# One kernel, one issue order: the order of all engines from a fixed table, and two first-tile pieces made into one

## The chip, the cores and the metric

The kernel runs on one core of a Trainium2 chip. The metric is the device time of one execution in microseconds (us). "Span" is the time from the first to the last instruction in a trace. All executions quoted here are at a granted TensorE clock of 0.997 to 1.000.

Engine names in the profile: PE is TensorE, PEld its weight loads, DVE is VectorE, ACT is ScalarE, POOL is GpSimd, SP is SyncE, which issues most DMAs (SPq).

## The reference, cut to what matters

```python
xn = _layernorm(x)                        # x: 1 x 2048 x 512, bf16
q, k, v = heads(xn@wq), heads(xn@wk), heads(xn@wv)   # paraphrased: 32 heads of 16, 4 segments of 512
for s in range(4):
    p = _softmax(qs @ ks.T * scale + mask)           # causal within the segment
    a_dot = p @ vs
    pq = phi(qs)                                     # phi(t) = t+1 if t>0 else exp(t)
    a_mem = (pq @ M) / (pq @ z + 1e-6)
    o = g * a_mem + (1.0 - g) * a_dot
    M, z = M + phi(ks).T @ vs, z + phi(ks).sum()
return x + concat(o) @ wo + silu(xn @ w1) @ w2       # w1: 512 x 1792, w2: 1792 x 512
```

## The kernel before

All work is written as tasks, each on one engine, with dependencies and with buffers that it takes and frees. A small scheduler in Python decides, while the program is built, in which order each engine issues its tasks. At run time each engine only follows its list. In the kernel before, the scheduler simulates the engines and picks by due times, which a table named SHIFT corrects by hand.

```python
            if e == "PE":
                s = [t for t in c if t.kind == "score"]
                if s:
                    return min(s, key=lambda t: t.seq)
# ... cut: PV blocks, ScalarE's and VectorE's rules
            return min(c, key=lambda t: (t.due, t.seq))
# ... cut
                    if t.lock:
                        other = "DVE" if e == "POOL" else "POOL"
                        d += max(0.0, port[other] - now)
                        port[e] = now + d
```

The last four lines matter later: the simulation holds a VectorE task marked `lock` while a GpSimd task marked so runs, and the other way round.

The heads of the first key and query tiles are made in four pieces of 128 columns each, so that the first scores can start early:

```python
        for j in (2 * hf, 2 * hf + 1):
            c, o = slice(j * P, (j + 1) * P), slice((j % 2) * P, (j % 2) * P + P)
            def f(c=c, o=o):
                for ki in range(DT):
                    mm(b.tile[:, o], w[:, ki, 0:P], xnT_b[0].tile[:, ki, c], ki == 0, ki == DT - 1)
            pcs.append(A("PE", 0.3, f, [xnT_done[0][j], loads], due + 0.01 * j, takes=(b,),
                         frees=(b, xnT_b[0]), mode="full", label=label))
```

The normalisation of the attention output multiplies by R, which comes back through DRAM. It is the task `a_t`, four per segment (three in the last).

```python
            def f_a(dt=dt, rb=rb):
                v = N_b[s].tile[:, dt, :]
                nc.vector.tensor_tensor(out=v, in0=v, in1=rb.tile[:], op=ALU.mult)
            a = A("DVE", 0.34, f_a, [d4] + mg, due_rep, frees=(rb, N_b[s]), label="a_t", lock=True)
```

The softmax here doesn't subtract the row's maximum and nothing guards it: scores larger than these inputs give would overflow.

Of the kernel before, what the change touches and what calls it, by code (L numbers as in the profile page):

```python
# [14 lines left out]
P = 128  # L15
# [25 lines left out]
STARVE = 0.55  # L41
# [4 lines left out]
LOWB = 1  # L46
# [8 lines left out]
LAST = 1  # L55
PVW = 0.0
# [9 lines left out]
SW = 0.1  # L66
SEM = 0.05
SHIFT = {
    "POOL": {
        ("", 4): -31.1, ("kB", 16): 80.6, ("pq", 0): -10.1, ("pq", 2): 18.3, ("pq", 6): 8.4,  # L70
        ("pq", 10): 6.2, ("M52", 1): -7, ("Mbf", 2): 35.4,
    },
    "PE": {
        ("tr", 1): 9.5, ("k1", 0): -13.1, ("k2", 0): 22.9, ("q2", 0): -12.4, ("q3", 0): -0.3,
        ("h0.0", 0): -54.5, ("h0.2", 0): 30.1, ("h0.3", 0): -7.3, ("h0.6", 0): 11.6,
        ("h0.7", 0): 10.6, ("h0.12", 0): -10.2, ("k4", 0): -0.9, ("q6", 0): 9.6, ("k7", 0): -11.8,
        ("v10", 0): -5.8, ("v11", 0): -6.8, ("M0", 0): 5, ("w2.1", 0): 1.8, ("w2.3", 0): -1.8,
        ("wo.3", 0): 20.3, ("h1.1", 0): 7.4, ("h1.3", 0): -16.4, ("h1.4", 0): 3.5,
        ("h1.5", 0): 1.8, ("h1.6", 0): 10.2, ("h1.7", 0): -10.6, ("h1.8", 0): -3.7,
        ("k8", 0): -7.8, ("v22", 0): -12.9, ("M1", 0): -7, ("psN", 0): -5.6, ("w2.4", 0): -30.2,  # L80
        ("w2.7", 0): -3.9, ("wo.4", 0): 28.9, ("wo.5", 0): 3.2, ("wo.6", 0): -27.6,
        ("wo.7", 0): -42.5, ("PV8", 0): 5.8, ("PV9", 0): 8.6, ("PV10", 0): 7.3, ("h2.0", 0): -7.2,
        ("h2.1", 0): 10.7, ("h2.5", 0): -7.9, ("h2.6", 0): -13.3, ("h2.9", 0): 7.9,
        ("q12", 0): -2.8, ("q13", 0): 4.8, ("k14", 0): 1.6, ("k15", 0): 15, ("v32", 0): 26.1,
        ("M2", 0): 29, ("w2.10", 0): 4, ("wo.9", 0): -27.9, ("wo.10", 0): 17.9, ("PV12", 0): 31.2,
        ("PV13", 0): 47.7, ("h3.0", 0): -14.7, ("h3.1", 0): 46.3, ("h3.2", 0): 38.7,
        ("h3.4", 0): -37.3, ("h3.7", 0): 26.5, ("h3.10", 0): -7.1, ("h3.12", 0): 16.4,
        ("h3.13", 0): 40.6, ("outT2", 0): -24.2,
    },
    "DVE": {  # L90
        ("stats", 3): 4.5, ("stats", 10): -3.1, ("xn", 5): -0.9, ("k0", 0): 11.1,
        ("EO", 26): 36.4, ("glu", 45): -20.7, ("tailA", 1): 4.6,
    },
    "SP": {
        ("Z", 15): -16.3, ("Z", 26): 8.7, ("den", 12): -6.9, ("den", 17): 3.5, ("den", 18): -28.9,
        ("den", 20): -20.5, ("out", 10): 21.7, ("mg", 14): 26.1,
    },
}


class Task:
    __slots__ = (
        "eng", "dur", "vis", "fn", "due", "nwait", "ready", "outs", "takes", "frees", "kind",
        "mode", "seq", "started", "end", "tvis", "label", "lock",
# [19 lines left out]
class Ring:  # L124
# [4 lines left out]
    def count(self, t):  # L129
        return sum(1 for a in self.at if a <= t + 1e-9)  # L130

    def take(self, t):
        i = min(range(len(self.at)), key=lambda k: self.at[k])
        assert self.at[i] <= t + 1e-9
        self.at[i] = float("inf")
        return i


class Sched:
    ENGS = ("SP", "ACTQ", "PE", "ACT", "DVE", "POOL")  # L140

    def __init__(self):
        self.tasks = []
        self.log = None
        self.names = {}

    def add(self, eng, dur, fn, deps=(), due=0.0, vis=None, seqdeps=(), takes=(), frees=(),
            kind="", mode=None, keep=0, label="", lock=None):
        t = Task()
        t.eng, t.dur, t.fn, t.due, t.kind, t.mode = eng, dur, fn, due, kind, mode  # L150
# [11 lines left out]
        t.started = False  # L162
        t.seq = len(self.tasks)
        t.label = label
# [9 lines left out]
    def shift(self, table):  # L174
        seen = {}
        for t in self.tasks:
            key = (t.eng, t.label)
            if t.eng == "PE" and t.label not in ("k0", "q0", "tr"):
                n = 0
            else:  # L180
                n = seen.get(key, 0)
                seen[key] = n + 1
            t.due += table.get(t.eng, {}).get((t.label, n), 0.0)

    def run(self):
        free = {e: 0.0 for e in self.ENGS}
        pool = {e: [] for e in self.ENGS}
        for t in self.tasks:
            if t.nwait == 0:
                pool[t.eng].append(t)  # L190
        port = {"DVE": 0.0, "POOL": 0.0}
        left = len(self.tasks)
        now = 0.0
        order = []
        st = {"mode": "full", "exp_next": None, "exps": 0}
        nexps = sum(1 for t in self.tasks if t.kind == "exp")

        def can(t):
            return all(b.idx is not None or b.ring.count(now) > keep for b, keep in t.takes)

        def pick(e):
            c = [t for t in pool[e] if t.ready <= now + 1e-9 and can(t)]
            if not c and e == "PE" and LAST:
                c = [
                    t for t in pool[e] if t.ready <= now + 1e-9 and t.kind == "" and all(
                        b.idx is not None or b.ring.count(now) > 0 for b, _ in t.takes)
                ]
            if not c:
                return None
            if e == "PE":  # L210
                s = [t for t in c if t.kind == "score"]
                if s:
                    return min(s, key=lambda t: t.seq)
                pv = [t for t in c if t.kind == "pv"]
                if not pv and any(
                    t.kind == "pv" and t.ready <= now + 1e-9 and t.due + PVW < now for t in pool[e]
                ):
                    c = [t for t in c if not any(
                        b.idx is None and b.ring is self.names["banks"] for b, _ in t.takes)]
                    if not c:  # L220
                        return None
                if pv:
                    b = min(pv, key=lambda t: (t.due, t.seq))
                    if st["mode"] != "full" or b.due < now:
                        return b
                    c = [t for t in c if t.kind != "pv"]
                    if not c:
                        return b
                return min(c, key=lambda t: (t.due, t.seq))
            if e == "ACT":  # L230
                s = [t for t in c if t.kind == "exp"]
                if s:
                    return min(s, key=lambda t: t.seq)
                b = min(c, key=lambda t: (t.due, t.seq))
                if st["exps"] < nexps and st["exp_next"] is not None:
                    late = 0.06
                    if not any(
                        t.kind != "score" and t.ready <= now + 1e-9 and can(t) for t in pool["PE"]
                    ):
                        late = STARVE  # L240
                    if now + b.dur > st["exp_next"] + late:
                        return None
                return b
            if e == "DVE":
                bk = self.names["banks"]
                if bk.count(now) <= LOWB:
                    f = [t for t in c if any(b.ring is bk for b in t.frees)]
                    if f:
                        return min(f, key=lambda t: (t.due, t.seq))
            return min(c, key=lambda t: (t.due, t.seq))  # L250

        while left:
            for e in self.ENGS:
                while free[e] <= now + 1e-9:
                    t = pick(e)
                    if t is None:
                        if e == "PE" and self.log is not None:
                            self.log.append((now, [
                                (x.label, round(x.ready, 1), [n for n, r in self.names.items() for b, k in x.takes if b.ring is r and b.idx is None and r.count(now) <= k])
                                for x in sorted(pool["PE"], key=lambda x: (x.due, x.seq))[:6]]))  # L260
                        break
                    pool[e].remove(t)
                    d = t.dur
                    if e == "PE":
                        if t.mode != st["mode"]:
                            d += SW
                            st["mode"] = t.mode
                        else:
                            pass
                    if t.lock:  # L270
                        other = "DVE" if e == "POOL" else "POOL"
                        d += max(0.0, port[other] - now)
                        port[e] = now + d
                    t.started = True
                    t.end = now + d
                    t.tvis = now + t.vis + (d - t.dur)
                    free[e] = t.end
                    for b, keep in t.takes:
                        if b.idx is None:
                            b.idx = b.ring.take(now)  # L280
# [1198 lines left out]
```

## Time and profile before

The time is 226.51 us, the median of 3 executions (226.26 to 226.98). The attention loop consists of 72 score blocks S0 to S71. Each is a short burst of row-tiled matmuls, followed on TensorE by about ten 512-column matmuls, or by a block of the attention's PV product, or by both. If one knows what each kind costs, the start times of the 72 blocks give a ledger: whatever an interval lasts beyond its content is a stall. The prediction derives the five unit costs from the intervals.

| part of the span, before | us |
|---|---|
| to S0 | 11.43 |
| S0 to S71, work | 187.35 |
| S0 to S71, stalls (S23 0.81, S27 0.42, S28 0.58, S42 0.55, S46 0.84, S47 0.27, S49 0.21, S62 0.14, rest -0.1) | 3.72 |
| after S71, work on TensorE | 19.51 |
| last eviction and output | 3.49 |
| span | 225.5 |

A stall of "S28" is time lost between the start of block 28 and that of block 29.

### The profile page before, as it was taken

To read this page: it belongs to the slowest core of one execution; us is meant where nothing else is said; L and a number is where in the kernel's file an instruction comes from. 1 tells how busy PE (TensorE), PEld (TensorE's weight loads), DVE (VectorE), ACT (ScalarE), POOL (GpSimd) and SP (SyncE) were. 2 spreads that over 40 slices of the span, in tenths; PEclk is the share of its full clock that TensorE was granted. 3 is DMA by queue.
4 is the path that set the end of the run, shared out by engine and by line. 5 is a ranking of instruction groups with operands and counts; after the bars stand their busy time and mean duration, and the time that the engine had idled before them with its cause. 6 is when DMAs were issued, how large, how long until landed. Compare 5 with 4: busy or idle time off the path is not lost.

```text
span 225.5 us, 6740 instructions
## 1 busy us (share of the span) xinstructions
PE 213.4 (95%) x2757; PEld 101.1 (45%) x2792; DVE 173.2 (77%) x305; ACT 179.7 (80%) x165; POOL 162.3 (72%) x283
## 2 busy tenths in 40 slices
PE   6899999999999898999999999999999999999994
PEld 6634444435443444444444334344554444444441
DVE  3788988879994789789976849988665784775873
ACT  4498999999988799988989787899898787994000
POOL 4779998889987678999984775968797644568100
PEclk9999999999999999999999999999999999999999
DMA  6974458550265432050364350020523201123202
GB/s 191 366 235 115 99 143 208 65 177 3 47 86 126 93 102 100 22 166 1 49 149 86 71 96 24 0 73 6 178 60 69 97 3 47 55 76 89 74 3 94
DMA packets 30708, 21.11 MB, mean 94 GB/s; under 512 B 15956, under 2 KB 29780, under 8 KB 30676
## 3 DMA queue, kind: packets, MB, share of 16 engines
q1 hardware_dynamic: 29860, 20.14, 34.4%
q10 hardware_dynamic: 816, 0.52, 0.8%
q8 instruction: 22, 0.36, 0.7%
q14 instruction: 10, 0.08, 0.1%
HBM read 11.73 MB, written 2.64 MB: 64 GB/s over the span
## 4 chain that ended last, share of the span: by engine, by line
PE 66%; DVE 8%; ACT 7%; DMA 7%; POOL 5%; issue 4%; SPq 1%; ACTq 0%; POOLq 0%
PE ps L583 54%; PE psS L583 11%; ACT Pt L947 6%; DMA phiK<-pkT 2%; POOL Pt L966 2%; DMA dR<-Zr 2%; DMA R<-dR 1%; POOL kB L824 1%; DMA x_all<-in_A_x_dram 1%; DVE xn L696 1%; DVE pq L760 1%; POOL rstd L685 1%; ACT hT L1239 1%; DVE st L662 1%; DMA Zg<-dZ 1%
## 5 line engine op out<-in xcount | busy, mean ns | idle before, releaser
L947 ACT ACTIVATE Pt<-psS 128x2048 bf16<-128x2048 f32 x72 | 135.4, 1880 | 18.3 <-PE psS L583 15.3
L966 POOL TENSOR_SCALAR_AFFINE_SELECT Pt<-Pt 64x512 bf16<-64x512 bf16 (+1 forms) x144 | 91.2, 634 | 29.3 <-ACT Pt L947 22.1
L583 PE MATMUL ps<-xnT,w 128*128 128x512 bf16 x214 | 57.0, 380 | 0.8 <-issue 0.5
L1243 DVE SCALAR_TENSOR_TENSOR hT<-hT,ps 128x512 bf16<-128x512 bf16 x56 | 36.9, 676 | 15.6 <-ACT hT L1239 15.4
L583 PE MATMUL ps<-w,hT 128*128 128x512 bf16 x185 | 46.6, 380 | 1.5 <-issue 1.4
L1239 ACT ACTIVATE hT<-ps 128x512 bf16<-128x512 f32 x56 | 32.1, 601 | 0.3 <-PE ps L583 0.3
L583 PEld LDWEIGHTS <-hT 128*128 128x128 bf16 x224 | 20.2, 98 | 24.5 <-issue 2.0
L583 PE MATMUL psS<-qT,kB 32*128 32x256 bf16 (+5 forms) x640 | 28.7, 261 | 1.7 <-ACT Pt L947 1.3
L583 PEld LDWEIGHTS <-w 128*128 128x128 bf16 x224 | 19.7, 98 | 23.3 <-issue 2.4
L583 PEld LDWEIGHTS <-kB 32*128 32x128 bf16 x640 | 12.0, 92 | 28.8 <-issue 27.2
L824 POOL TENSOR_SCALAR kB<-kT,pm 128x512 bf16<-128x512 bf16 x30 | 21.8, 736 | 4.1 <-DVE kT L819 2.6
L583 PE MATMUL ps<-Pt,V 64*32 64x256 bf16 (+5 forms) x640 | 19.8, 260 | 0.2 <-DVE N L1224 0.2
L583 PE MATMUL ps<-Pt,VS 64*32 64x256 bf16 (+5 forms) x640 | 18.8, 261 | 0.2 <-DVE acc L1268 0.2
L583 PE MATMUL ps<-xnT,w_q 128*128 128x512 bf16 (+1 forms) x73 | 17.3, 345 | 0.7 <-DVE xnT L724 0.5
L583 PE MATMUL ps<-xnT,w_k 128*128 128x512 bf16 (+1 forms) x73 | 17.3, 344 | 0.5 <-DVE hT L1243 0.4
L583 PEld LDWEIGHTS <-V 64*32 64x32 bf16 x640 | 14.1, 91 | 7.8 <-issue 2.5
L583 PE MATMUL ps<-w_v,xnT 128*128 128x512 bf16 x61 | 15.8, 380 | 0.4 <-issue 0.3
L1145 POOL TENSOR_TENSOR pq<-pq,Dr 128x512 bf16<-128x512 bf16 x12 | 14.1, 1182 | 1.8 <-DMA Dr<-dE 1.2
L583 PE MATMUL ps<-w_o,N 128*128 128x512 bf16 x51 | 14.5, 380 | 0.4 <-issue 0.3
L760 DVE SCALAR_TENSOR_TENSOR pkT<-kT,pkT 128x512 bf16<-128x512 bf16 x12 | 11.6, 963 | 2.2 <-POOL pkT L754 2.2
L1023 DVE CAST N<-ps 128x512 bf16<-128x512 f32 x15 | 10.2, 682 | 3.9 <-PE ps L583 3.8
L583 PEld LDWEIGHTS <-VS 64*32 64x32 bf16 x640 | 12.7, 91 | 0.7 <-DVE acc L1268 0.5
(104 smaller groups left out, 251.4 us busy)
## 6 DMA issues: line engine op xcount, KB each, us to landing
w<-in_B_w_dram SPq DMA_DIRECT2D x4, 896.0 KB
VS<-V SPq DMA_DIRECT2D x8, 264.0 KB
out_dram<-o_t SPq DMA_DIRECT2D x16, 128.0 KB
R<-dR SPq DMA_DIRECT2D x15, 128.0 KB
Dr<-dE SPq DMA_DIRECT2D x12, 128.0 KB
x_all<-in_A_x_dram SPq DMA_DIRECT2D x2, 512.0 KB
N<-O SPq DMA_DIRECT2D x12, 64.0 KB
w_k<-in_A_wk_dram SPq DMA_DIRECT2D x2, 256.0 KB
```

Of the source, the lines that this page charges most:

```text
L583: nc.tensor.matmul(o, lhsT=l, rhs=r, start=start, stop=stop, **k)
L662: nc.vector.bn_stats(out=b.tile[:], in_=xt(t))
L685: nc.gpsimd.tensor_tensor(out=rs, in0=mv[:, t : t + n, 1:2] if first else rs, in1=lnc[:, 0:n, 1:2], op=ALU.pow,)
L696: nc.vector.tensor_scalar(out=xb.tile[:], in0=xt(t), scalar1=mv[:, t, 0:1], scalar2=rstd[:, t, 0:1], op0=ALU.subtract, op1=ALU.mult,)
L760: nc.vector.scalar_tensor_tensor(out=dst_b.tile[:], in0=src_b.tile[:], scalar=0.0, in1=dst_b.tile[:], op0=ALU.max, op1=ALU.add, accum_out=acc,
L824: nc.gpsimd.tensor_scalar(out=kB[u].tile[:, :, KB * r : KB * r + KB], in0=kT[u].tile[:].rearrange("p (a b) -> p a b", b=KB), scalar1=pm[:, ...
L947: nc.scalar.activation(out=pb.tile[:], in_=psS[:], func=AF.Exp, scale=SCALE)
L966: nc.gpsimd.affine_select(out=v, in_=v, compare_op=ALU.is_ge, fill=0.0, base=0, pattern=pat, channel_multiplier=-1,)
L1023: nc.vector.tensor_copy(out=dst.tile[:, dt, :], in_=buf.tile[:])
L1145: nc.gpsimd.tensor_tensor(out=pb.tile[:], in0=pb.tile[:], in1=rb.tile[:], op=ALU.mult)
L1239: nc.scalar.activation(out=hb.tile[:], in_=b.tile[:], func=AF.Tanh, scale=0.5)
L1243: nc.vector.scalar_tensor_tensor(out=hb.tile[:], in0=hb.tile[:], scalar=1.0, in1=b.tile[:], op0=ALU.add, op1=ALU.mult)
```

## The change

The intent is to fix every engine's order, found elsewhere, in a table that the builder simply follows. The second half of the first key and query tiles becomes one piece of 256 columns. The change is also described as putting the loads first on ScalarE's queue, but ScalarE's program begins with the same rows before and after. The diff, cut to its core:

```diff
-SHIFT = { "POOL": {("", 4): -31.1, ...}, "PE": {...}, "DVE": {...}, "SP": {...} }
+ORDER = """ ... """            # 1699 task numbers, about 80 lines, cut
     def run(self):
-        while left:
-            for e in self.ENGS:
-                while free[e] <= now + 1e-9:
-                    t = pick(e)            # due times, priorities; cut
+        for k in ORDER.split():
+            t = self.tasks[int(k)]
+            assert t.nwait == 0
     def first_tile(w, loads, due, label, hf):
-        for j in (2 * hf, 2 * hf + 1):
+        for js in ((0,), (1,)) if hf == 0 else ((2, 3),):
+            n = len(js)
-            c, o = slice(j * P, (j + 1) * P), slice((j % 2) * P, (j % 2) * P + P)
+            c, o = slice(js[0] * P, (js[0] + n) * P), slice((js[0] % 2) * P, (js[0] % 2 + n) * P)
-            pcs.append(A("PE", 0.3, f, [xnT_done[0][j], loads], ...
+            pcs.append(A("PE", 0.3 if n == 1 else 0.44, f, [xnT_done[0][j] for j in js] + [loads], ...
```

## The prediction

> **What bounds the kernel now.** I read the page first (busy shares and the 40 slices), then the chain that ended last, then TensorE's rows in order of time, then the waits, and last the first 12 us.
>
> The page, parts 1 and 2: busy us and share by engine, then busy tenths in 40 slices.
>
> ```profile
> PE 213.4 (95%) x2757; PEld 101.1 (45%) x2792; DVE 173.2 (77%) x305; ACT 179.7 (80%) x165; POOL 162.3 (72%) x283
> PE   6899999999999898999999999999999999999994
> ACT  4498999999988799988989787899898787994000
> ```
>
> TensorE is the bound from slice 3 to the end; no other engine is near it throughout. But busy overstates a pipelined TensorE, so I need its real pace. The chain, one regular stretch and two disturbed ones (start us, us, what):
>
> ```profile
> 30.15 0.33 PE psS L583 x12
> 30.48 2.27 PE ps L583 x10
> 32.74 0.33 PE psS L583 x12
> 33.08 2.26 PE ps L583 x10
> ...
> 69.09 4.49 DMA phiK<-pkT
> 73.67 0.63 ACT pkT L751
> 74.30 1.77 ACT Pt L947
> ...
> 130.91 3.31 DMA R<-dR
> 134.59 0.68 DVE N L1224
> ```
>
> The loop is 72 score blocks S0 to S71, each followed by about ten 512-column matmuls. From the score rows of TensorE's timeline I took the start of each block (S0 11.43 us, S71 202.50 us) and from the instruction order what stands between them. The intervals with ten matmuls last 2.595 us and those with eleven 2.81, so a matmul costs 0.2155 us and a score block with both mode switches 0.44. Intervals with a PV block of the attention give 1.14 us for it, a denominator block 0.33, a 128-column memory matmul 0.065. These five numbers reproduce nearly every interval within 0.02 us. What is left over is **TensorE's stalls: 3.9 us in all** (191.07 measured, 187.17 of work), nearly all in few places: S23 0.81, S27 0.42, S28 0.58, S42 0.55, S46 0.84, S47 0.27, S49 0.21, S62 0.14. The waits view names two causes (total, times, longest, us):
>
> ```profile
> DVE N L1209 <- DMA R<-dR: 4.4, 4, 2.6
> ACT pkT L751 <- DMA phiK<-pkT: 0.9, 1, 0.9
> ```
>
> S23 is ScalarE stuck in front of an exponential, waiting for a transpose DMA to release a buffer. S42 to S47 lie around VectorE standing at the normalisation, which waits for the reciprocals to come back through DRAM; PSUM banks stay full behind it. S27 and S28 are neither: they hold only 7, and 1 plus a PV block (1.95 and 1.80 us of TensorE work), less than ScalarE's round of 2.38 us, so TensorE starves.
>
> The ledger of the 225.5 us span: 11.43 to S0, 187.17 of work, 3.9 of stalls, 19.47 after S71 (83 full matmuls, one PV, one score block), 3.5 for the last eviction and output DMA. The sum is 225.5. The timed median is 1.0 above the profiled span.
>
> The start, in order of time:
>
> ```profile
> 8.88 0.40 PE L709 MATMUL ps<-ident,xn 128*128 128x128 bf16 x4
> 9.43 0.42 DVE L808 CAST kT<-ps 128x256 bf16<-128x256 f32 x1 [0.28 <-ACT kB L798]
> 9.77 0.41 DVE L724 COPY xnT<-ps 128x512 bf16<-128x512 bf16 x1
> 10.24 0.38 PE L583 MATMUL ps<-xnT,w_q 128*128 128x128 bf16 x4 [0.51 <-DVE xnT L724]
> 10.66 0.37 ACT L856 CAST qT<-ps 128x256 bf16<-128x256 f32 x1 [1.26 <-PE ps L583]
> 11.43 0.40 PE L583 MATMUL psS<-qT,kB 32*128 32x512 bf16 x4
> ```
>
> The fourth transpose is done at 9.28, but VectorE first copies kT, so xnT comes 0.45 us late and TensorE idles 0.51.
>
> **What the Trainium skill says.** "Perfetto Trace Analysis", section Identifying the Most-Contended Engine, says matmul busy share is no good measure of headroom. This trace agrees: 95% busy leaves 12 us by the page, but the intervals leave 3.9. "TensorE: Matmul & The Clock Gate", section Step-by-step, gives about 216 ns between 512-column matmuls and says that matmuls stay in program order and no other engine reorders; the trace has 0.2155 us, and the 2.6 us VectorE wait with ready work behind it fits in-order issue. "DMA: Bandwidth & Descriptors", section Issuing engines are not separate DMA queues, says that issuing from a second engine saves only sequencer time. Here ScalarE spends 0.91 and 0.46 us on its load issues, ready by 2.2, while its first computation waits for data until 4.14.
>
> **The change, part by part.**
>
> Loads on ScalarE's queue first: the built ScalarE program begins with the same rows before and after (two x loads, w_q, table load, mean, square). Cost and gain 0.
>
> Second halves in one piece: per tile, two pieces of four 128-column matmuls (about 57 ns each, 0.46) become four of 256 columns (estimate: half of 0.2155, so 0.43). Eight matmuls and weight loads fewer, 0.05 us gained, but the piece must now wait for tile 3. The new order puts two v matmuls into that wait, and moves the xnT copy ahead of the qT and kT copies. Worked through: xnT 9.33 to 9.74, query piece 9.78 to 10.21, key piece to 10.64, two more v matmuls to 11.07, mode switch 0.1: **S0 at about 11.2**, 0.25 earlier, with four v matmuls behind it instead of three of k1. All 26 warm-up pairs now stand ahead of the first transpose; ten more small matmuls at 72 ns push it from 5.76 to about 6.3. The third and fourth transposes wait for VectorE until 7.98 and 8.88, so I expect that to vanish.
>
> The table: the same work, so only three things can change. Work: S0 to S71 now holds 187.38, the tail 19.04 (81 matmuls); together 206.42 against 206.64. Mode runs stay 165. Stalls: three changes in the order address the causes one by one. (a) On SyncE the transpose behind S23 now stands ahead of the Z and VS transfers it was queued behind. (b) On VectorE the distance from the reciprocal to the first normalisation grows from 7 to 14 operations in the second segment and from 4 to 8 in the third; at some 0.66 us each, 14 last about 9 us, nearly what the trip through DRAM took before (reciprocal 124.0, R landed 134.2). In the first it stays at 11. (c) The smallest interval holds 2.44 us of TensorE work against 1.80 before, so it no longer falls under ScalarE's 2.38. Where ScalarE has two extra activations its work (1.77 an exponential, 0.48 a tanh, 0.52 another exponential) exceeds TensorE's: 14 intervals, 2.0 us in sum. The kernel before has 13 such, also 2.0 us, beside S27 and S28, and they show 0.2 us of stalls, so neighbours absorb it.
>
> Sum with no stall: 11.2 + 206.42 + 3.5 = 221.1, plus 1.0 for timed against profiled: **222.1 us**. I allow 1.0 us of stalls that stay or are new: **223.1 us**, 1.5% faster.
>
> **Rivals.**
> Stalls change place. SyncE issues in order and its list is reshuffled everywhere; a transfer that waits holds all behind it. The masks on GpSimd are now taken out of order (M3, M1, M4), a PV block waits for its last mask. For: the order was made without this trace, 3.9 us is already little, and four banks leave no slack. Against: the three changes above hit just the places that stalled. It would give 225 to 227.
> No stall at all: 222.1. If interleaving the 128-column memory matmuls with wide ones also shortens them (48 times 0.01), and the start gains more, 221.6, just past 2%. For it speaks the even filling; against, that all must go right together.
> The start or tail loses: warm-ups delay the first copies, or VectorE's new end (both tail reciprocals and products, then three a_t, three oT) gives the last output projections late. By instruction durations the first oT comes 14.3 us after S71 and its first reader is due at about 14.3: up to 0.5 us, so 223.6.
>
> **Range and chances.** Below is the floor: 222.1, with 0.1 for errors of the terms. Above, half of the old stalls come back and the start gains nothing: 222.1 + 2.0 + 0.5 + some noise, 225.0. A factor of 0.98 is 221.98, just under the no-stall figure: chance of faster 0.09. Slower by 2% means 231.0, with nine us of new stalls: 0.02. The rest is within 2%.
>
> **What would show it.** S0 near 11.2 and xnT directly after the fourth transpose; score blocks at 2.595 with ten matmuls; the time from S0 to S71 near 188.4 (187.4 of work); no wait of ScalarE's pkT for the phiK transfer; VectorE's wait for R under 2 us in total; the end 22.5 after S71. I am wrong if S0 to S71 stays near 191 (new stalls took the old ones' place), if matmuls pace differently, or if S0 comes later than 11.43.

## The result, and the profile after

| kernel | median us | range | executions |
|---|---|---|---|
| before | 226.46 | 226.26 to 226.98 | 6 |
| after | 226.41 | 226.01 to 226.92 | 6 |

The ratio is 0.9996, with a 95% interval from 0.9979 to 1.0012: the same. A ratio is the mean time of one kernel's fast runs over that of the other's of the same rounds, so it is not quite the ratio of the medians quoted. The result is correct against the reference. The prediction expected 223.1 us and a range from 222.0 to 225.0. A change within 2%, which it held likeliest, came true. The time fell outside the range.

Part 1 of the page of the changed kernel: busy us (share of the span) by engine.

```profile
PE 217.6 (97%) x2784; PEld 101.4 (45%) x2784; DVE 172.3 (77%) x305; ACT 180.5 (80%) x165; POOL 162.2 (72%) x283
```

TensorE looks fuller, 97% against 95%, and yet the time is equal. That is a warning about this figure: the busy time went up by 4.2 us while the work went slightly down. The trace of before has 2757 matmuls beside 2792 weight loads, so 35 matmul records are missing there and none here. I did not work out whether that is all of the difference.

The chain that ended last, for the changed kernel (start us, us, what): a regular interval and two disturbed places.

```profile
14.31 0.33 PE psS L506 x8
14.64 2.26 PE ps L506 x10
16.90 0.33 PE psS L506 x12
...
73.96 3.71 DMA Zg<-dZ
77.69 0.95 DVE Zf L1106
...
185.92 2.33 DVE pq L683 x2
```

The regular intervals are what they were, 2.59 us from one score block to the next with ten matmuls between (16.90 minus 14.31). The transfers of phiK and R have left the chain. Another transfer, Zg, and a VectorE operation stand in it now. The waits view of the changed kernel (total, times, longest, us) has no wait for R and none for phiK. It has this one:

```profile
DVE Zf L1106 <- DMA Zg<-dZ: 3.9, 3, 2.8
```

The timeline at that place shows how the wait reaches TensorE (start us, us, engine, line, operation, idle time before and its releaser):

```profile
73.96 0.54 SPq L1095 DMA_DIRECT2D Zg<-dZ  x1
...
77.69 0.95 DVE L1106 RECIPROCAL Zf<-Zg 128x128 f32<-128x128 bf16 x1 [2.75 <-DMA Zg<-dZ]
...
78.76 0.68 DVE L1167 SCALAR_TENSOR_TENSOR hT<-hT,ps 128x512 bf16<-128x512 bf16 x1
...
79.49 0.81 PE L506 MATMUL ps<-xnT,w 128*128 128x512 bf16 x3 [0.60 <-DVE hT L1167]
```

VectorE stands 2.75 us before a reciprocal. The gate step behind it in VectorE's list, the one on hT, could have run long before. It waited for nothing else: ScalarE had finished its input at 75.93. It alone would have freed the bank (one of the kernel's four PSUM buffers, named ps, into which matmuls write) that TensorE wants at 79.49. The second place, from the same timeline:

```profile
185.84 2.40 DVE L683 SCALAR_TENSOR_TENSOR pq<-qT,pq 128x512 bf16<-128x512 bf16 x2
...
187.05 0.40 PE L506 MATMUL psS<-qT,kB 32*128 32x256 bf16 x12
187.38 0.40 PE L506 MATMUL ps<-pq,zden 128*32 128x512 bf16 x3
188.29 0.38 PE L506 MATMUL ps<-pq,zden 128*32 128x512 bf16 x1 [0.52 <-DVE pq L683]
```

The denominator block stands right behind score block 66, and the query features that it reads are ready only at 188.24.

The start of the changed kernel, in order of time:

```profile
9.27 0.40 PE L632 MATMUL ps<-ident,xn 128*128 128x128 bf16 x4 [0.28 <-DVE xn L619]
...
9.77 0.42 DVE L647 COPY xnT<-ps 128x512 bf16<-128x512 bf16 x1 [0.56 <-PE ps L632]
...
10.25 0.60 PE L506 MATMUL ps<-xnT,w_q 128*128 128x256 bf16 x4
...
11.65 0.39 PE L506 MATMUL psS<-qT,kB 32*128 32x512 bf16 x4
```

The copy of xnT now follows the fourth transpose directly, as the prediction said, and 256-column pieces take the place of the 128-column ones. S0 is nevertheless at 11.65 and not at 11.2. The first tile of x arrived 3.66 us after the start of the span here and 3.27 us in the traced run of before. Over all fourteen traces it is 3.27 to 3.83 us.

The ledger of all traces, counted again with one set of unit costs. S0 minus x is counted from the arrival of the first tile of x:

| trace | S0 | S0 minus x | work S0 to S71 | stalls | after S71 | rest | span |
|---|---|---|---|---|---|---|---|
| before | 11.43 | 8.16 | 187.35 | 3.72 | 19.51 | 3.49 | 225.5 |
| after | 11.65 | 7.99 | 187.57 | 2.73 | 19.08 | 3.47 | 224.5 |

Stalls of after: S4 0.10, S5 0.12, S6 0.22, S8 0.12, S22 0.12, S24 0.38, S25 0.66, S50 0.13, S66 0.89. None of the eight places of before is among them. The old stalls went, and nearly as many new ones came.

### The profile page after: what moved, and what is told of

Its sections match the earlier page's. It is cut to its first block, busy times and chain, and to the rows that moved or that the text cites. A ratio compares the mean times of both kernels' runs of the same rounds, so it can differ in the third digit from the quotient of the medians.

```text
span 224.5 us, 6732 instructions
## 1 busy us (share of the span) xinstructions
PE 217.6 (97%) x2784; PEld 101.4 (45%) x2784; DVE 172.3 (77%) x305; ACT 180.5 (80%) x165; POOL 162.2 (72%) x283
## 4 chain that ended last, share of the span: by engine, by line
PE 79%; POOL 8%; DVE 5%; DMA 3%; ACT 2%; issue 1%; SPq 0%; POOLq 0%
PE ps L506 67%; PE psS L506 12%; POOL Pt L891 2%; POOL kB L749 2%; DMA Zg<-dZ 2%; ACT Pt L872 2%; POOL rstd L608 1%; DMA x_all<-in_A_x_dram 1%; POOL pq L677 1%; DVE pq L683 1%; DVE st L585 1%; DVE xn L619 1%; DVE hT L1167 1%; DVE Zf L1106 0%; POOL rstd L598 0%
## 5 line engine op out<-in xcount | busy, mean ns | idle before, releaser
L891 POOL TENSOR_SCALAR_AFFINE_SELECT Pt<-Pt 64x512 bf16<-64x512 bf16 (+1 forms) x144 | 89.7, 630 | 29.2 <-ACT Pt L872 24.2
L506 PE MATMUL ps<-xnT,w 128*128 128x512 bf16 x224 | 60.5, 380 | 0.6 <-DVE hT L1167 0.6
L506 PE MATMUL ps<-w,hT 128*128 128x512 bf16 x196 | 52.0, 380 | 0.0
L506 PEld LDWEIGHTS <-hT 128*128 128x128 bf16 x224 | 20.4, 98 | 25.8 <-issue 3.9
L506 PEld LDWEIGHTS <-w 128*128 128x128 bf16 x224 | 20.4, 98 | 24.2 <-issue 3.1
L506 PE MATMUL psS<-qT,kB 32*128 32x256 bf16 (+5 forms) x640 | 28.6, 262 | 0.0
L506 PEld LDWEIGHTS <-kB 32*128 32x128 bf16 x640 | 11.6, 92 | 26.1 <-issue 24.0
L506 PE MATMUL ps<-Pt,V 64*32 64x256 bf16 (+5 forms) x640 | 19.7, 260 | 0.0
L506 PE MATMUL ps<-Pt,VS 64*32 64x256 bf16 (+5 forms) x640 | 19.0, 261 | 0.2 <-DMA VS<-V 0.2
L506 PE MATMUL ps<-xnT,w_k 128*128 128x512 bf16 (+2 forms) x72 | 18.6, 356 | 0.4 <-ACT xnT L645 0.4
L506 PE MATMUL ps<-xnT,w_q 128*128 128x512 bf16 (+2 forms) x72 | 18.0, 356 | 0.2 <-issue 0.2
L506 PEld LDWEIGHTS <-V 64*32 64x32 bf16 x640 | 14.3, 91 | 8.3 <-issue 3.0
L506 PE MATMUL ps<-w_v,xnT 128*128 128x512 bf16 x64 | 17.8, 380 | 0.0
L506 PE MATMUL ps<-w_o,N 128*128 128x512 bf16 x54 | 15.0, 380 | 0.0
L585 DVE BATCH_NORM_STATS2 st<-x_all 128x6 f32<-128x512 bf16 x15 | 10.2, 681 | 3.7 <-DMA x_all<-in_A_x_dram 3.7
L506 PEld LDWEIGHTS <-VS 64*32 64x32 bf16 x640 | 12.8, 91 | 0.5 <-DMA VS<-V 0.5
L744 DVE CAST kT<-ps 128x512 bf16<-128x512 f32 x15 | 10.2, 682 | 3.5 <-PE ps L506 2.9
```

The lines of the kernel that those rows point to most:

```text
L506: nc.tensor.matmul(o, lhsT=l, rhs=r, start=start, stop=stop, **k)
L585: nc.vector.bn_stats(out=b.tile[:], in_=xt(t))
L744: ev = [A("DVE", 0.6, lambda: nc.vector.tensor_copy(out=kT[u].tile[:], in_=b.tile[:]), [g], due + 1.5, takes=(kT[u],), frees=(b, kT[u]), l ...
L891: nc.gpsimd.affine_select(out=v, in_=v, compare_op=ALU.is_ge, fill=0.0, base=0, pattern=pat, channel_multiplier=-1,)
```

## The experiments

All kernels give a correct result. Each was timed in five rounds beside before. The table of task numbers was edited, so most edits are shown as the change in one engine's list. Line numbers in their traces are lower by three than in the changed kernel (L503 is its L506). Times are medians in us. The three batches ran on three chips, so a time is best compared with the before of its own batch.

| batch | run | time | range | before on the same chip | ratio, 95% interval | stalls in the trace |
|---|---|---|---|---|---|---|
| 1 | before_again | 227.04 | 226.34 to 227.31 | 226.26 | 1.0030 [0.9997, 1.0064] | 2.93 |
| 1 | after_again | 226.80 | 226.46 to 228.35 | 226.26 | 1.0044 [1.0006, 1.0082] | 3.17 |
| 1 | merge_only | 227.13 | 225.39 to 227.79 | 226.26 | 1.0029 [0.9991, 1.0068] | 2.81 |
| 1 | no_merge | 228.75 | 228.56 to 229.07 | 226.26 | 1.0113 [1.0077, 1.0149] | 4.97 |
| 2 | after_third | 226.74 | 226.24 to 228.21 | 227.03 | 0.9995 [0.9963, 1.0026] | 3.50 |
| 2 | fix_den | 226.43 | 225.07 to 227.79 | 227.03 | 0.9973 [0.9933, 1.0012] | 4.13 |
| 2 | fix_zg | 227.62 | 227.14 to 227.85 | 227.03 | 1.0019 [0.9993, 1.0045] | 3.64 |
| 2 | fix_all | 226.45 | 224.45 to 227.17 | 227.03 | 0.9964 [0.9927, 1.0001] | 2.71 |
| 3 | after_fourth | 226.82 | 226.13 to 227.18 | 226.82 | 0.9987 [0.9949, 1.0024] | 2.71 |
| 3 | no_merge_lock | 227.53 | 226.53 to 228.16 | 226.82 | 1.0014 [0.9978, 1.0051] | 3.07 |
| 3 | fix_lock | 226.64 | 226.24 to 227.03 | 226.82 | 0.9980 [0.9946, 1.0013] | 2.86 |
| 3 | fix_all_lock | **224.64** | 224.53 to 225.26 | 226.82 | **0.9897** [0.9864, 0.9931] | **0.90** |

### The parts of the change: before_again, after_again, merge_only, no_merge

before_again takes before's own order, written down as a table, with no other difference. Its instruction streams are those of before.

```diff
-        the scheduler picks by due times
+        ORDER = the order that the scheduler of before had picked
```

> The kernel before, its order written as a table (the built instruction streams are identical, buffer numbers included): a control. Theory 'unlucky trace' (the traced run of before, 227.24 us, was 0.8 above its own median): median 226.4, spans of the timed runs near 224.5 and not 225.5, and a new trace shows S0 to S71 in about 190.3 us (3.1 of stalls) or S0 earlier than 11.4. Rival 'the trace is typical': spans near 225.5, 191.0 us from S0 to S71, 3.9 us of stalls again at S23, S27, S28, S42, S46.

The traced span was 225.2 us, with 2.93 us of stalls at seven of the old places. From S0 to S71 it took 190.28 us, as the theory of an unlucky trace said, while the spans of the timed runs, 224.6 to 225.6 us, reach from that theory's to the rival's. That the order comes from a table costs and gains nothing that these times resolve. It also shows the spread of one and the same program: 226.34 to 227.31 here, and 225.08 to 227.79 in the eleven executions of before in this batch. Single stalls that hang on DMA landings differ as well (S46 0.84 in one trace and 0.17 in the other).

after_again is the changed kernel, unedited.

> The changed kernel unaltered: a control. If its trace is typical: median 226.4, spans 224.1 to 224.9, S0 to S71 in 190.3 us with 2.9 of stalls, at S24/S25 (1.0) and S66 (0.9) again. If its start was unlucky (the first x tile landed at 3.66 us against 3.27 in the kernel before), a second trace has it near 3.3 and S0 near 11.3.

The same stalls came back at the same places, S66 at 0.89 again and S24 and S25 at 1.06 together. The first tile of x came at 3.50 us and S0 at 11.48, between the two cases. Two of six executions took 228.23 and 228.35 us, some 1.7 us more than the other four. They were not traced.

merge_only has before's order with the second halves in one piece.

```diff
-        for j in (2 * hf, 2 * hf + 1):
+        for js in ((0,), (1,)) if hf == 0 else ((2, 3),):
```

> The kernel before in its own order, with the second halves of the first key and query tiles in one piece (the later half's place): one part of the change alone. Theory 'the piece is worth nothing': time within 0.3 us of before, S0 within 0.15 us of it. Rival 'waiting for the fourth tile delays the first score': S0 0.3 to 0.5 us later and the time as much longer.

S0 minus x grew from 8.18 to 8.85 us: in the old order the one piece waits while VectorE copies other things first. The loop has about as much of stalls as before, at S27, S28, S42, S46, S49 and S62; the one at S23 is missing, and S42 has 1.22 us. The single piece without the new order costs 0.67 us at the start, more than the rival's 0.5. The time does not resolve that.

no_merge has the changed kernel's order with two pieces again. Of its engines' lists only TensorE's differs from that of the changed kernel, at the two pieces.

```diff
-        for js in ((0,), (1,)) if hf == 0 else ((2, 3),):
+        for js in ((0,), (1,)) if hf == 0 else ((2,), (3,)):
```

> The changed kernel with the second halves split again into two pieces at the same place: the change without that part. Theory 'worth nothing': within 0.3 us of the changed kernel. Rival 'it pays for the new start': 0.2 to 0.4 us longer, S0 later by as much (8 more small matmuls and weight loads of 57 ns at most).

S0 minus x was 8.01 against 7.98 us in after_again. The piece is worth 0.03 us there, as the prediction thought. And yet all four executions were near 228.75 us, 2 us above the changed kernel. The stalls were 4.97 us. Of these 2.12 us lay at S28, S29 and S30, where the changed kernel has nothing, and 0.68 at S9, whose cause I did not look for. A change in the first 12 us cannot cost 2 us at 87 to 97 us by its own work. This was the first hint of a switch in the loop that is thrown by a shift of some tenths of a microsecond.

### Taking away the new stalls one by one: after_third, fix_den, fix_zg, fix_all

after_third is the changed kernel as the base of this batch.

> The changed kernel once more, as the base of this batch. Both theories: 226.0 to 227.0 us median, stalls of 2.7 to 3.2 us between the first and the last score block, of them 0.89 before S66 counted with its block, about 1.05 at S24 and S25, and 0.3 to 0.6 at S4 to S8. A second group of executions some 1.7 us longer may show again.

It had 226.74 us, and 3.50 us of stalls in the trace, 0.71 of them at S6 and 0.37 at S2. S0 minus x was 8.27 us here, because TensorE waited 0.80 us for the key weights to land. One execution took 228.21 us.

fix_den moves one denominator product on TensorE:

```diff
 TensorE:
  S66
- den3
  w2 (nine matmuls)
+ den3
  S67
 VectorE:
- den, acc
+ acc, den
```

> The changed kernel with the last denominator product moved from right behind score block 66 to right ahead of score block 67, so that VectorE has one block more to finish the features of the query. Theory (a stall is worth its own length when nothing else waits there): the 0.89 us at S66 go, the time is 0.8 to 0.9 us below the changed kernel's of this batch. Rival (a stall taken away comes back at another place): S66 is free of a stall, but other blocks gain as much, and the time stays within 0.4 us.

The timeline of fix_den at S66 shows that the local effect is the expected one:

```profile
186.55 0.40 PE L503 MATMUL psS<-qT,kB 32*128 32x256 bf16 x12
186.88 2.33 PE L503 MATMUL ps<-w,hT 128*128 128x512 bf16 x9
189.15 0.40 PE L503 MATMUL psS<-qT,kB 32*128 32x256 bf16 x12
```

No idle time is left, and the stall of S66 is 0.00. The traced execution, one of the slower, has S28 0.44, S29 0.69 and S30 0.98 instead. The fastest three executions have spans of 223.4 to 223.9 us, about 0.9 below the 224.4 to 224.8 us of the changed kernel's four fastest in this batch. The other three were slower. The median is 0.31 us below the changed kernel's, within the rival's 0.4. If the fast executions are those without stalls at S28 to S30, the stall is worth its full 0.89, and a second thing of 2.1 us hides it in others. None of the fast ones was traced, and one slow execution (227.10 us) has a span of only 224.2, so not all of the scatter is this.

fix_zg changes the order on SyncE and moves one gate step on VectorE:

```diff
 SyncE:
- Z, Z, xnT, VS, mg, mg, VS
+ VS, VS, Z, Z, xnT, mg, mg
 VectorE:
- reciprocal Zr (waits for Zg), gcol, glu
+ glu, reciprocal Zr (waits for Zg), gcol
```

> The changed kernel with SyncE issuing both halves of the value sums of segment 1 ahead of the two transfers of the denominators, and one gating step on VectorE ahead of the reciprocal that waited 2.75 us for one of them. Theory: the 1.05 us at S24 and S25 go and nothing comes in their place, so the time is 0.9 to 1.1 us below the changed kernel's of this batch. Rival: the later denominators hold VectorE's reciprocal and what follows it as long as before, the stall moves to S26 to S30, and the time stays within 0.4 us.

S24 and S25 are free of stalls, as the theory said. But S28, S29 and S30 had 0.44, 0.69 and 0.98, a sum of 2.11, and all six executions took over 227.1 us. The median is 0.88 us above the changed kernel's, so the rival's 0.4 us failed like the theory. Stalls did come at S28 to S30, among the blocks that the rival named. Their cause is the subject of the next runs.

fix_all is both edits and a third, at S6:

```diff
  (fix_den and fix_zg, and:)
 TensorE in block 6:
- q4 (four matmuls), PV0
+ PV0, q4 (four matmuls)
 VectorE:
- qT, EO, EO
+ EO, EO, qT
```

> Both edits together, and in block 6 the product of values ahead of the fourth query projection that waited for the transposed input, with two exponentials' follow-up steps on VectorE ahead of the query copy. Theory: the stalls fall from about 2.9 to 0.5 to 1.0 us and the time is 1.9 to 2.4 us below the changed kernel's of this batch, near 224.4 us, which is what the prediction's allowance of 1.0 us of stalls meant. Rival: the order is so tight that each shift makes new waits; stalls stay above 2 us, and the time within 0.8 us.

The stalls of S6, S24, S25 and S66 are all gone. The sum is 2.71 nevertheless, and 2.11 of it lie again at S28 to S30, to the hundredth as in fix_den and fix_zg. One execution took 224.45 us, the others 225.90 to 227.17. The median is 0.3 us below the changed kernel's. By both of its numbers the rival came true. But a stall of always the same size, on or off, is no chaos of small shifts. It asks for one cause.

### The switch at S28 to S30: no_merge_lock, fix_lock, fix_all_lock, after_fourth

The timeline of no_merge, at S28 to S30, with rows of TensorE and other operations between them left out:

```profile
87.35 0.69 POOL L746 TENSOR_SCALAR kB<-kT,pm 128x512 bf16<-128x512 bf16 x1
87.48 0.83 DVE L1130 TENSOR_TENSOR N<-N,R 128x512 bf16<-128x512 bf16 x1 [0.31 <-DMA R<-dR]
...
90.21 0.61 POOL L674 TENSOR_SCALAR pkT<-pkT 128x512 bf16<-128x512 bf16 x1
90.24 0.85 DVE L1130 TENSOR_TENSOR N<-N,R 128x512 bf16<-128x512 bf16 x1
...
92.55 1.47 POOL L888 TENSOR_SCALAR_AFFINE_SELECT Pt<-Pt 64x512 bf16<-64x512 bf16 x2 [1.73 <-ACT Pt L869]
92.83 1.47 DVE L1130 TENSOR_TENSOR N<-N,R 128x512 bf16<-128x512 bf16 x1
...
94.22 0.68 DVE L789 CAST qT<-ps 128x512 bf16<-128x512 f32 x1
94.95 0.59 PE L503 MATMUL ps<-w_o,N 128*128 128x512 bf16 x2 [0.65 <-DVE qT L789]
```

And the same operations in the changed kernel:

```profile
87.20 0.43 DVE L1133 TENSOR_TENSOR N<-N,R 128x512 bf16<-128x512 bf16 x1
87.30 0.88 POOL L749 TENSOR_SCALAR kB<-kT,pm 128x512 bf16<-128x512 bf16 x1
...
89.55 0.41 DVE L1133 TENSOR_TENSOR N<-N,R 128x512 bf16<-128x512 bf16 x1
89.86 0.61 POOL L677 TENSOR_SCALAR pkT<-pkT 128x512 bf16<-128x512 bf16 x1 [0.30 <-ACT pkT L674]
91.68 0.42 DVE L1133 TENSOR_TENSOR N<-N,R 128x512 bf16<-128x512 bf16 x1
...
92.10 1.26 POOL L891 TENSOR_SCALAR_AFFINE_SELECT Pt<-Pt 64x512 bf16<-64x512 bf16 x2 [1.63 <-ACT Pt L872]
```

The multiplication N by R is one and the same instruction, of 0.41 to 0.43 us here and of 0.83 to 1.47 us there. Where GpSimd has started 0.03, 0.13 or 0.28 us earlier, the multiplication ends 0.27 or 0.28 us after GpSimd's work ends. Where the multiplication starts first, it lasts 0.41 to 0.43 us, and GpSimd's kB, if it starts meanwhile, takes 0.88 us instead of 0.69. The Trainium skill, "SBUF — State Buffer", section Who interferes with whom, says that a VectorE instruction with two SBUF inputs contends with a GpSimd instruction that reads SBUF. In its line on VectorE's two-port modes it adds that whoever issues first has the shared ports for the whole instruction while the other fully blocks. The traces agree in kind. In size the multiplication ends 0.27 us after GpSimd's work, less than the 0.41 us that it takes alone; the traces do not say why. The slack is small: in the changed kernel the third multiplication starts 0.31 us ahead of GpSimd and the fourth 0.42 us. In no_merge the third comes 0.03 us behind it, a relative shift of 0.34 us. Its delay of 0.44 us then puts the fourth behind GpSimd as well. VectorE copies qT and frees its PSUM bank later, and TensorE stands.

The chain begins at the second multiplication, and there a transfer has a part. In no_merge it waited 0.31 us for R to land, and so came behind GpSimd's kB. The gate step and the reciprocal behind it came later too, and with them the third multiplication. All eight traces with this place of VectorE's list sort the same way. In the four with the 2.1 us (no_merge, fix_den, fix_zg, fix_all) the second multiplication waited 0.31 to 0.54 us for R and started 0.13 to 0.46 us after kB. In the four of the changed kernel VectorE stood idle at most 0.11 us before it, and it started 0.02 to 0.21 us before kB. So R's landing seems to throw the switch, which is read from eight traces and not tested by an edit. At the third and fourth multiplication, S29 and S30, VectorE had no idle time before them, and the lock alone makes them long.

What I changed is one place of VectorE's list. The gate step and the reciprocal no longer stand behind a multiplication that waits for R. The third and fourth multiplication go into a stretch in which GpSimd is idle, behind both evictions.

```diff
 VectorE:
- a_t(2), glu, reciprocal Dg, kT, a_t(3), O, N, phi, a_t(4), qT
+ glu, reciprocal Dg, a_t(2), kT, O, N, a_t(3), a_t(4), phi, qT
```

no_merge_lock has this in no_merge:

> The run with the second halves in two pieces, with VectorE's order changed at one place alone: the gate step and the reciprocal ahead of the second multiplication by R, and the third and fourth multiplication behind both evictions. Lock theory (these multiplications read two SBUF operands and wait out whatever the pool engine has begun; 0.41 us alone, 0.83, 0.85 and 1.47 in the slow case): they take under 0.6 us each, the 2.1 us of stalls at S28 to S30 go, and the time falls from 228.7 to about 226.7 us. Rival (these blocks wait for the late transfer of R itself): the same stalls stay, at most 0.5 us is gained.

The four multiplications took 0.55, 0.36 and, as a pair, 0.75 us. S28 and S29 had no stall, S30 0.19. The ratio to before went from 1.0113 to 1.0014, and the median to 227.53, 1.2 us less than no_merge on another chip. The traced execution was the fastest, 226.53 us. The median is 0.8 above what was expected, and I have no trace of a slower execution. So the lock is shown as the cause of the stalls at S29 and S30 in the trace, and as one part of that at S28: there the edit also takes the gate step out from behind the wait for R. The last 0.8 us of the median stay unexplained; 0.41 us at S9 are in the trace.

fix_lock has it in the changed kernel alone:

> The changed kernel with that same one place of VectorE's order changed. Lock theory: its usual executions, which had no stall at S28 to S30, stay at 226.0 to 227.0 us, and those near 228.3 do not occur. Rival: both kinds occur as before.

It had 226.64 us, 226.24 to 227.03, and stalls of 2.86 us at the changed kernel's places, S24, S25 and S66. No execution was near 228.3, but none of the base was either. The base of this batch is the changed kernel again:

> The changed kernel as the base of this batch. All theories: 226.0 to 227.0 us for most executions, a few near 228.3, which would be those where the normalisation of the third tile meets the pool engine's work (2.1 us of stalls at S28 to S30).

It had 226.82 us, at most 227.18, and stalls of 2.71 us. So fix_lock says that this order costs nothing where the switch is off, and that the earlier gate step by itself gains nothing there. Whether the three executions of after_again and after_third above 228.2 us were the switch stays open, because none of them was traced.

fix_all_lock has it in fix_all:

> The run with all three edits (last denominator product, value sums first on SyncE, block 6), with that same place changed as well. Lock theory: S28 to S30 lose 2.1 us, stalls are 0.3 to 0.8 us in all, the median is 224.2 to 224.8 us, 1.7 to 2.4 us below the changed kernel of this batch. Rival: other blocks gain in turn, the median stays above 225.5 us.

The median is 224.64 us, 224.53 to 225.26, against 226.82 for both the changed kernel and before on this chip. The ratio to before is 0.9897, and all six executions lie below all eleven of before. The traced span is 222.7 us with 0.90 us of stalls: S4 0.10, S5 0.12, S22 0.17, S30 0.19, S50 0.13, S60 0.13. Its timeline at S29 and S30:

```profile
88.66 0.61 POOL L674 TENSOR_SCALAR pkT<-pkT 128x512 bf16<-128x512 bf16 x1 [0.55 <-ACT pkT L671]
89.77 0.75 DVE L1130 TENSOR_TENSOR N<-N,R 128x512 bf16<-128x512 bf16 x2
90.90 1.35 POOL L888 TENSOR_SCALAR_AFFINE_SELECT Pt<-Pt 64x512 bf16<-64x512 bf16 x2 [1.63 <-ACT Pt L869]
```

Both multiplications now lie in GpSimd's gap from 89.27 to 90.90, with 0.4 us to spare. This version beats both kernels by 1%: clear of the noise. The one fast execution of fix_all, 224.45 us, had the same span of 222.7 us without the lock edit. So the edit does not make the best execution faster. It makes it the usual one. It differs from the changed kernel in order alone.

## Why the prediction was right or wrong

The failed step is "I allow 1.0 us of stalls that stay or are new: 223.1 us". The changed kernel has 2.7 to 3.5 us in four traces. The prediction's first rival, "Stalls change place", with 225 to 227 us, is what happened, and its own test said so in advance: "I am wrong if S0 to S71 stays near 191". It was 190.30.

Part of the old 3.9 us was the execution too. The traced execution of before took 227.24 us, 0.7 above its median, and the trace of before_again has 2.93 us of stalls. Against that the changed kernel's 2.7 to 3.5 us are no gain.

Point by point, from the traced execution of 226.37 us:

- **The named cures worked.** The stalls of before at S23, S27, S28, S42 to S49 and S62 are zero in the changed kernel. No wait for phiK and no wait for R is in its waits view (predicted: under 2 us for R). That fits reasons (a), (b) and (c), but no run changed one of them alone.
- **The new stalls were not looked for.** I had followed only the operations that stalled before. For the new order I had the issue lists of all engines. In them the reciprocal that waits for Zg stands ahead of a gate step that needs nothing of it, the second half of the value sums VS stands on SyncE behind a transpose and two other transfers, and den3 stands directly behind S66 with its features two VectorE operations away. All three were readable. The three cost 1.9 us together (S24, S25, S66), shown by the edits that took them away. The rest is at S4 to S8, S22 and S50. Against the allowance that is 2.73 instead of 1.0: **+1.73 us**.
- **Timed against profiled, "plus 1.0".** The span of before, 225.5 us, belongs to an execution that itself took 227.24 us, so the difference is 1.74. I had set it against the median of other executions. For the changed kernel it is 1.87: **+0.87 us**. This error was avoidable: both numbers belonged to one and the same execution, whose own time was listed.
- **S0 "at about 11.2".** 11.65, **+0.45 us**. Its mechanism is right (xnT directly after the transpose, S0 minus x 0.17 us shorter where 0.25 was expected). The rest is the arrival of x: 3.27 us in before's trace, the earliest of fourteen, and 3.66 in after's, one of the four latest. The middle one is 3.48. I took a lucky landing for the rule, and the result's trace had an unlucky one.
- **Work.** 187.57 with the fitted costs, where 187.38 was expected: +0.19. The recount raised before's work by 0.18 in the same way, so in the prediction's own count these 0.19 us are stalls, 2.92 in all. Tail and end 19.08 and 3.47 for 19.04 and 3.5: no error. The unit costs held.
- **Sum.** 1.73 + 0.87 + 0.45 + 0.19 + 0.01 = 3.25, and 223.12 + 3.25 = 226.37, the traced execution.
- **Loads, warm-ups and the single piece** were called near zero. The piece is worth 0.03 us in the new order (no_merge against after_again, S0 minus x). The later transposes at 8.37 and 9.27 are as late as x was, 0.39 us each, so the warm-ups ahead of the first did not delay them. The first did come later, at 6.78 instead of 5.76.
- **Rival "no stall at all"** needed what the changed kernel lacks. fix_all_lock nearly has it. With S0 at 11.69 and 0.90 us of stalls it ends at a span of 222.7. The prediction's ledger for 1.0 us of stalls, with the start and the offset corrected, is 223.12 + 0.87 + 0.45 + 0.19 = 224.6, and its measured median is 224.64. With these three terms taken from the measurement, the arithmetic was good for the kernel that the prediction imagined.
- **Why the chances were off.** The range's upper end assumed that half of the old stalls come back. About three quarters of the 3.72 us came back in the result's trace, at other places. And a switch of 2.1 us, the port lock, was only 0.02 to 0.21 us away in the changed kernel's four traces. It has no part in the 226.41 us, whose trace has nothing at S28 to S30, but no sum of single delays contains it.

## What to carry to other kernels

Where one engine is 97% full, a new order is not judged by the stalls that it removes: go through each engine's new list and ask of every operation that waits for a transfer what stands behind it. Count stalls by intervals of the bounding engine, because the busy share rose by two points here while nothing was gained. When a stall is on or off with one fixed size, look for a lock: put two-input VectorE operations into stretches where GpSimd is idle, with some tenths of a microsecond to spare, and compare a span only with the time of the same execution.

## What the Trainium skill lacked or had wrong

- "SBUF — State Buffer", section Who interferes with whom, was right, but it speaks of single instructions. I found no page that says that such a lock can put a whole program in one of two timings. Here it stretched one multiplication from 0.41 to 1.47 us, through two GpSimd instructions in a row (0.86 and 0.65 us), and stalls of 2.1 us (0.44, 0.69 and 0.98 at S28 to S30) came or not with a shift of some tenths of a microsecond.
- "TensorE: Matmul & The Clock Gate", section Back-to-back issue gap, gives for streams of weight load and matmul about 131 ns a matmul at 512 columns, and says that the isolated gap over-counts. The regular intervals of these traces show 0.2155 us with a weight load for every matmul, and so the isolated gap that the page gives as well (about 216 ns).
- "TensorEngine Tiling (Array Packing)", section Tiling Modes, says that a change of the tiling mode drains TensorE, and gives no size. A score block costs 0.44 us in the intervals and 0.33 us of that is its own row in the chain, so both changes together take about 0.11 us (an estimate from these two numbers).
- I found no page that gives the step from the span, first to last instruction, to the device time of the same execution. It was 1.7 to 2.1 us in nearly all executions here, with a few at 2.2 to 2.9.
